# GpSimd's products of the causal convolution: tensor times one scalar per partition in place of tensor times a stretched weight

## The chip, the cores and the metric

The kernel runs on one core of a Trainium2 chip. A core has several engines with queues of their own: TensorE (PE in the profile; its weight loads are listed apart as PEld), VectorE (DVE), ScalarE (ACT), GpSimd (POOL) and SyncE (SP), which here issues most DMAs. Each engine works through its own list of instructions in order; semaphores hold an instruction until what it reads is there. The metric is device time in microseconds (us) of one execution. The numbers for the kernel before are from three timed runs and one profiled execution.

## The reference, cut to what matters

An attention with a causal mask and a decay bias (batch 8, heads 8, 576 tokens, 64 per head) gives `x` of 576 tokens by 512 channels per batch. It goes through a gated linear unit whose gate is a causal depthwise convolution of five taps:

```python
xp = np.concatenate([np.zeros((B, K - 1, D)), x], axis=1)
gate_pre = np.zeros((B, S, D))
for k in range(K):                                   # K = 5
    gate_pre += conv_w[k][None, None, :] * xp[:, k:k + S, :]
gate = 1.0 / (1.0 + np.exp(-gate_pre))
val = x @ w_val
return gate * val @ w_out
```

For one channel a tap is one number for all tokens. In the kernel channels lie on partitions and tokens along them, so a tap is one scalar per partition.

## The kernel before, in words

The work is cut into 32 units `n` (8 batches of 4 pairs of heads; a pair of heads is 128 channels, one full set of partitions). For each unit the kernel loads Q, K and V, casts Q and K to bf16 (`c_q`, `c_k`), transposes them on TensorE (`qt`, `qq`) and copies them out of PSUM (`qe`); TensorE makes scores (`s0` to `s2`, `s4`), ScalarE their exponentials (`e0` to `e2`, `e4`), GpSimd masks the diagonal blocks of some units (`mk`, `ml`, L580) and multiplies V by the exponential of the decay (`vp`, L475); TensorE multiplies by V (`av0`, `av`, L595), VectorE normalises (`rec`, `nm`), and TensorE turns the result so that channels lie on partitions (`xt`, L627). That result stands in PSUM as bf16 and is copied to SBUF as `xT` (`xe`).

The convolution of unit `n` then runs over up to 576 tokens. `t1` (L666, VectorE) adds tap 1 to the unshifted value; the weights are divided by the last tap beforehand (`cwr`), so that the last tap costs nothing here. Taps 2, 3 and 4 come either from VectorE in one instruction, product and sum (L671), or from GpSimd in two: a product `p2`, `p3` or `p4` written to one of two buffers `pr` in f32, and the sum `t2`, `t3` or `t4` of `gp` and `pr` (L674). Some products are made by ScalarE (L653). The function of the products is `tap_product`. ScalarE then takes the tanh (`th`), TensorE the value product (`val`, L704), VectorE the gate times the value (`glu`), and TensorE the output product (`out`, L724). The last batch (units 28 to 31) is done in two halves of 384 and 192 tokens, with shorter products.

What runs where and in which order is written out by hand in one long string, `ORDER`: a list of steps `name.index:engine:buffer`, where G is GpSimd, V VectorE, A ScalarE, T TensorE and S SyncE. Each engine's instructions are issued in the order of that list. GpSimd's list has 29 products, 37 sums, 32 products of V, 19 masks and 16 casts, one after the other; a piece of it around units 5 and 6 reads (other engines' steps left out):

```
t2.5:G  cast_wo:G  t3.5:G  p3.6:G:0  mk.9:G  p4.5:G:1  t3.6:G  t4.5:G  vp.2.0:G
```

Of the kernel before, what the change touches and what calls it, by code (L numbers as in the profile page):

```python
# [12 lines left out]
ALU = mybir.AluOpType  # L13
# [284 lines left out]
def main_path(ctx, tc, q, k, v, s, moe_w_val, moe_conv_w, moe_w_out, out, okcnt):  # L298
# [6 lines left out]
    vec, act, pool, sync, pe = nc.vector, nc.scalar, nc.gpsimd, nc.sync, nc.tensor  # L305
# [35 lines left out]
    xTs = many("xT", [128, 4, 4 + S], BF16)  # L341
# [304 lines left out]
    def tap_product(m):  # L646
        def f(e, n, *h):
            b, c = divmod(n, 4)
            lo, hi = span(*h)
            lo = max(lo, m)  # L650
            pr, r = prs[at[f"p{m}", n, *h][0]][:, lo:hi], cwr[:, c, 4 - m:5 - m]
            if e is act:
                act.activation(out=pr, in_=xps(n, *h)[:, lo - m:hi - m], func=AF.Copy, scale=r)  # L653
            else:
                pool.tensor_tensor(pr, xTs[b % 2][:, c, 4 + lo - m:4 + hi - m], r.to_broadcast([128, hi - lo]),  # L655
                                   ALU.mult)
        return f

    def tap(m):
# [181 lines left out]
```

## Time and profile before

| what | value |
| --- | --- |
| median of three runs | 189.03 us (188.85 to 191.28) |
| time of the profiled execution | 188.3 us |
| span of the profiled execution, first to last instruction | 186.5 us |
| busy: PE, ACT, DVE, POOL | 173.7, 171.3, 165.3, 162.1 us |
| GpSimd's products (L655) | 29, 29.7 us busy |
| GpSimd's sums (L674) | 37, 46.1 us busy |
| ScalarE's products of the same kind (L653) | 8 |

The span lies 1.8 us under the time of its execution, and that execution 0.7 us under the median of the runs. Busy times are sums over the span; an engine's list is in order, so an engine that is busy nearly throughout can make others late even where the chain that ended last doesn't name it.

### The profile page before, as it was taken

The numbers are of one execution on the slowest core, as the hardware profiler recorded it, in microseconds if no ns is written. First come the engines' busy times: TensorE is split into PE (matmuls) and PEld (weight loads), VectorE is DVE, ScalarE is ACT, GpSimd is POOL, SyncE is SP. The second block draws the span as 40 slices with busy tenths as digits, with TensorE's granted clock in tenths as the row PEclk, the third lists the DMA queues.
The fourth block names the chain that finished last, engine by engine and source line by source line (L and its number), as shares of the span: only waits on it lengthen the run. The fifth ranks groups of instructions, "written<-read, shape, count | busy, mean of one in ns | idle before, by whom it ended". The sixth has DMA issues, their size and how long they took to land.

```text
span 186.5 us, 6691 instructions
## 1 busy us (share of the span) xinstructions
PE 173.7 (93%) x2735; PEld 114.3 (61%) x2735; DVE 165.3 (89%) x320; ACT 171.3 (92%) x233; POOL 162.1 (87%) x145
## 2 busy tenths in 40 slices
PE   6999797889999999999979999999999999999991
PEld 2547574377757665576845676486666865667560
DVE  4876989879998899998999999989999899999980
ACT  3399979999999989999999989999999999999871
POOL 5049999998999999999999999799999988799530
PEclk9999999999999999999999999999999999999998
DMA  5999999899899999997999992899970003403064
GB/s 181 238 292 317 241 270 195 235 361 302 173 303 350 396 250 251 257 339 193 301 201 241 330 295 75 251 292 283 201 248 3 4 5 112 169 5 116 2 225 176
DMA packets 62283, 40.46 MB, mean 217 GB/s; under 512 B 47333, under 2 KB 49381, under 8 KB 62250
## 3 DMA queue, kind: packets, MB, share of 16 engines
q1 hardware_dynamic: 61706, 39.49, 76.8%
q8 instruction: 22, 0.36, 0.8%
q10 hardware_dynamic: 544, 0.52, 0.8%
q14 instruction: 11, 0.09, 0.2%
HBM read 30.57 MB, written 9.44 MB: 214 GB/s over the span
## 4 chain that ended last, share of the span: by engine, by line
PE 72%; ACT 18%; DVE 4%; issue 3%; POOL 0%; ACTq 0%; POOLq 0%; DVEq 0%
PE bank L704 15%; PE bank L724 15%; PE bank L595 13%; ACT P L557 13%; PE bank L506 11%; PE bank L621 6%; PE bank L627 4%; PE bank L630 3%; PE bank L490 2%; PE bank L519 1%; PE bank L481 1%; ACT ot L374 1%; DVE gp L666 1%; DVE gp L671 1%; ACT th L691 1%
## 5 line engine op out<-in xcount | busy, mean ns | idle before, releaser
L557 ACT ACTIVATE P<-bank 128x1024 bf16<-128x1024 f32 x84 | 83.2, 1044 | 3.3 <-PE bank L506 1.9
L671 DVE SCALAR_TENSOR_TENSOR gp<-bank,cwr,gp 128x574 f32<-128x574 bf16 (+6 forms) x71 | 51.2, 743 | 0.3
L674 POOL TENSOR_TENSOR gp<-gp,pr 128x572 f32<-128x572 f32 (+6 forms) x37 | 46.1, 1249 | 4.8 <-DVE gp L671 2.9
L506 PE MATMUL bank<-QKT 64*128 64x128 bf16 (+4 forms) x592 | 38.1, 237 | 4.5 <-ACT P L557 2.5
L475 POOL TENSOR_TENSOR Vp<-vst,w 128x650 bf16<-128x650 f32 x32 | 40.6, 1288 | 0.2 <-ACT w L395 0.2
L704 PE MATMUL bank<-xT,wv 128*128 128x288 bf16 (+2 forms) x256 | 38.2, 286 | 0.9 <-DVE gp L671 0.5
L595 PEld LDWEIGHTS <-P 128*128 128x128 bf16 x960 | 33.2, 97 | 6.0 <-issue 1.6
L595 PE MATMUL bank<-Vp,P 128*128 128x65 bf16 x960 | 36.2, 194 | 0.8 <-ACT P L557 0.6
L724 PE MATMUL bank<-wo,glu 128*128 128x512 bf16 x144 | 36.0, 380 | 0.0
L506 PEld LDWEIGHTS <-QKT 64*128 64x128 bf16 x592 | 19.3, 94 | 22.1 <-issue 16.4
L655 POOL TENSOR_TENSOR pr<-xT,cwr 128x572 f32<-128x572 bf16 (+6 forms) x29 | 29.7, 1031 | 2.0 <-DVE xT L374 0.9
L704 PEld LDWEIGHTS <-wv 128*128 128x128 bf16 x256 | 22.5, 97 | 9.9 <-issue 3.8
L713 DVE SCALAR_TENSOR_TENSOR glu<-th,bank 128x288 bf16<-128x288 f32 (+2 forms) x64 | 26.9, 446 | 1.7 <-ACT th L691 0.5
L666 DVE SCALAR_TENSOR_TENSOR gp<-xT,cwr,bank 128x576 f32<-128x576 bf16 (+2 forms) x36 | 26.6, 743 | 1.2 <-ACT xT L374 0.2
L614 DVE TENSOR_TENSOR xn<-bank,recs 128x640 bf16<-128x640 f32 (+2 forms) x36 | 26.9, 747 | 0.7
L580 POOL TENSOR_SCALAR_AFFINE_SELECT P<-P 128x1024 bf16<-128x1024 bf16 (+2 forms) x19 | 19.2, 1011 | 9.2 <-ACT P L557 9.1
L374 ACT COPY QKT<-bank 128x1024 bf16<-128x1024 bf16 (+1 forms) x21 | 20.9, 1027 | 2.2 <-PE bank L490 2.1
L691 ACT ACTIVATE th<-gp,cwr 128x576 f32<-128x576 f32 x28 | 21.8, 799 | 0.0
L724 PEld LDWEIGHTS <-glu 128*128 128x128 bf16 x144 | 12.1, 98 | 12.6 <-issue 1.9
L374 ACT COPY ot<-bank 128x512 f32<-128x512 f32 x29 | 17.2, 610 | 1.8 <-PE bank L724 1.7
L374 DVE COPY QKT<-bank 128x1024 bf16<-128x1024 bf16 (+1 forms) x15 | 14.5, 972 | 3.7 <-PE bank L490 2.4
L627 PE MATMUL bank<-ident,xn 128*128 128x128 bf16 x164 | 15.0, 220 | 0.9 <-ACT P L557 0.6
(66 smaller groups left out, 184.2 us busy)
## 6 DMA issues: line engine op xcount, KB each, us to landing
out_dram<-ot SPq DMA_DIRECT2D x36, 256.0 KB, 3.1
vst<-in_v_dram SPq DMA_DIRECT2D x28, 256.0 KB, 6.4
first<-in_q_dram SPq DMA_DIRECT2D x6, 512.0 KB, 6.8
first<-in_k_dram SPq DMA_DIRECT2D x6, 512.0 KB, 7.4
qkf<-in_q_dram SPq DMA_DIRECT2D x6, 512.0 KB, 7.1
qkf<-in_k_dram SPq DMA_DIRECT2D x6, 512.0 KB, 6.7
vst<-in_v_dram SPq DMA_DIRECT2D x15, 128.0 KB, 4.8
first<-in_q_dram SPq DMA_DIRECT2D x4, 256.0 KB, 4.0
```

Source lines behind the costliest of these rows:

```text
L374: (act.copy if e is act else e.tensor_copy)(dst, src)
L475: e.tensor_tensor(Vps[b % 2][:, :, HP[p]], vslot(b)[:, :, HP[p]], w[:, :, b * 8 + 2 * p:b * 8 + 2 * p + 2].unsqueeze(3).to_broadcast([128, ...
L506: pe.matmul(ps[:, hh, c0:c0 + nq], QKTs[b % 2][r, 1, p, k0:k0 + 128], QKTs[b % 2][r, 0, p, q0:q0 + nq], **kw)
L557: act.activation(out=Pt(n)[:, :, step * 512:(step + 1) * 512], in_=pair((f"s{step}", n)), func=AF.Exp, scale=0.125)
L595: pe.matmul(ps[:, o:o + 65], lhsT, Vps[b % 2][:, kb, 2 * p + w, :], start=(kb == 0), stop=(kb == qb))
L614: vec.tensor_tensor(xns[b % 2][:, g, p * 128:(p + 1) * 128].rearrange("t g (w d) -> t w g d", w=2), ps[:, :, :, 0:64], recs[:, n, :, g].un ...
L655: pool.tensor_tensor(pr, xTs[b % 2][:, c, 4 + lo - m:4 + hi - m], r.to_broadcast([128, hi - lo]), ALU.mult)
L666: vec.scalar_tensor_tensor(gp[:, lo:hi], xT[:, 3 + lo:3 + hi], r, xps(n, *h)[:, lo:hi], ALU.mult, ALU.add)
L671: vec.scalar_tensor_tensor(gp[:, lo:hi], xps(n, *h)[:, lo - m:hi - m], r, gp[:, lo:hi], ALU.mult, ALU.add)
L674: pool.tensor_tensor(gp[:, lo:hi], gp[:, lo:hi], prs[at[f"p{m}", n, *h][0]][:, lo:hi], ALU.add)
L704: pe.matmul(ps, wv[:, dc, c * 128:(c + 1) * 128], xTs[b % 2][:, dc, 4 + lo:4 + hi], start=(dc == 0), stop=(dc == 3))
L724: pe.matmul(bank_of(u, i), glu2[:, c, i * 128:i * 128 + 128], wo[:, c, :], start=(c == 0), stop=(c == 3))
```

## The change

In `tap_product`, the branch for GpSimd changes. Before, it is `tensor_tensor`: two tensor operands, the second being the weight `r` (one f32 number per partition) stretched over the 192 to 574 tokens by a step of zero. After, it is `tensor_scalar`: one tensor operand, and `r` given as the scalar operand, one f32 per partition; its second operation is left empty. Input (bf16 `xT`), output (f32 `pr`), the numbers of elements, the buffers and `ORDER` stay as they are. ScalarE's branch and the sums stay too.

```diff
             if e is act:
                 act.activation(out=pr, in_=xps(n, *h)[:, lo - m:hi - m], func=AF.Copy, scale=r)
             else:
-                pool.tensor_tensor(pr, xTs[b % 2][:, c, 4 + lo - m:4 + hi - m], r.to_broadcast([128, hi - lo]),
-                                   ALU.mult)
+                pool.tensor_scalar(pr, xTs[b % 2][:, c, 4 + lo - m:4 + hi - m], r, None, ALU.mult)
         return f
```

## The prediction

> **What bounds the kernel now.** I read the busy shares first, then the chain that ended last, and then asked what GpSimd's list, which the change touches, does to that chain.
>
> ```profile
> PE 173.7 (93%) x2735; PEld 114.3 (61%) x2735; DVE 165.3 (89%) x320; ACT 171.3 (92%) x233; POOL 162.1 (87%) x145
> PE 72%; ACT 18%; DVE 4%; issue 3%; POOL 0%; ACTq 0%; POOLq 0%; DVEq 0%
> ```
>
> The first line is busy time and its share of the span by engine, the second the shares of the chain. TensorE carries the chain and ScalarE most of the rest; GpSimd has nothing in it. So a faster GpSimd has nothing of its own to take off the end. That doesn't make a slower GpSimd free: the table of two stretches (from:to, length, then each engine's busy us) shows how full it is.
>
> ```profile
> 20.00:140.00 120.00, 113.34 (x1971) 76.16 (x1970) 111.18 (x194) 116.60 (x148) 117.30 (x91) 1.00 0.97 263
> 140.00:180.00 40.00, 39.83 (x556) 26.94 (x551) 38.79 (x90) 38.28 (x64) 34.07 (x36) 1.00 0.19 68
> ```
>
> The columns of busy time are PE, PEld, DVE, ACT, POOL. From 20 to 140 us GpSimd is busy for 117.30 of 120 us, more than any other engine there, and idles for 2.7; from 140 to 180 it idles for 5.9. The view of waits says who is kept waiting by it, and whom it waits for (total us, times, longest).
>
> ```profile
> PEld L595 <- POOL Vp L475: 0.7, 1, 0.7
> ACT P L557 <- POOL pr L655: 0.3, 1, 0.3
> PE bank L595 <- POOL Vp L475: 0.2, 1, 0.2
> ...
> POOL P L580 <- ACT P L557: 9.1, 3, 5.7
> POOL gp L674 <- DVE gp L671: 2.9, 4, 1.7
> POOL gp L674 <- DVE gp L666: 1.2, 2, 0.8
> POOL pr L655 <- DVE xT L374: 0.9, 2, 0.6
> POOL pr L655 <- ACT xT L374: 0.7, 1, 0.7
> ```
>
> Others wait for GpSimd for 1.2 us in all. The timeline (start, length, engine, line) shows what these waits are worth, and how near the others come:
>
> ```profile
> 22.96 1.28 POOL L475 TENSOR_TENSOR Vp<-vst,w 128x650 bf16<-128x650 f32 x1
> 23.30 1.05 ACT L557 ACTIVATE P<-bank 128x1024 bf16<-128x1024 f32 x1
> 24.49 0.70 PE L595 MATMUL bank<-Vp,P 128*128 128x65 bf16 x18 [0.41 <-ACT P L557]
> ...
> 26.41 0.40 PE L506 MATMUL bank<-QKT 64*128 64x128 bf16 x8
> 26.91 2.13 ACT L557 ACTIVATE P<-bank 128x1024 bf16<-128x1024 f32 x2 [0.30 <-POOL pr L655]
> ...
> 35.60 3.76 POOL L475 TENSOR_TENSOR Vp<-vst,w 128x650 bf16<-128x650 f32 x3
> 36.94 1.08 PE L595 MATMUL bank<-Vp,P 128*128 128x65 bf16 x30
> 38.17 0.49 PE L595 MATMUL bank<-Vp,P 128*128 128x65 bf16 x11 [0.16 <-POOL Vp L475]
> 48.33 1.89 POOL L374 CAST wo<-qkf 128x2048 bf16<-128x2048 f32 x1
> 50.27 1.02 PE L724 MATMUL bank<-wo,glu 128*128 128x512 bf16 x4
> 178.95 0.59 POOL L674 TENSOR_TENSOR gp<-gp,pr 128x192 f32<-128x192 f32 x1 [0.46 <-DVE gp L671]
> 179.72 0.41 DVE L671 SCALAR_TENSOR_TENSOR gp<-bank,cwr,gp 128x192 f32<-128x192 bf16 x1
> ```
>
> The wait of 0.7 us, of a weight load, ends with the product of V at 22.96 + 1.28 = 24.24, but the matmul behind it also needs exponentials that end at 24.35. The one of 0.3 us is followed by an exponential at 26.91 whose scores are only done at 26.81. That leaves the 0.2 us, at 38.17.
>
> The output weights are cast by 48.33 + 1.89 = 50.22, and TensorE's first output product starts at 50.27: 0.05 us later. The last sum on GpSimd ends at 179.54, 0.18 us before VectorE goes on with that `gp`. A delay of GpSimd reaches TensorE almost at once, and TensorE, busy for 113 of 120 us, hardly catches up.
>
> **The change, part by part.** It swaps 29 instructions; none is added, moved or dropped, no DMA and no wait. Those removed, by shape (count | busy us, mean ns | idle before):
>
> ```profile
> L655 POOL TENSOR_TENSOR pr<-xT,cwr 128x572 f32<-128x572 bf16 x10 | 11.4, 1140 | 0.2
> L655 POOL TENSOR_TENSOR pr<-xT,cwr 128x574 f32<-128x574 bf16 x7 | 8.0, 1142 | 1.0 <-DVE xT L374 0.9
> L655 POOL TENSOR_TENSOR pr<-xT,cwr 128x573 f32<-128x573 bf16 x5 | 5.7, 1139 | 0.0
> L655 POOL TENSOR_TENSOR pr<-xT,cwr 128x380 f32<-128x380 bf16 x2 | 1.6, 818 | 0.0
> L655 POOL TENSOR_TENSOR pr<-xT,cwr 128x192 f32<-128x192 bf16 x3 | 1.5, 505 | 0.8 <-ACT xT L374 0.7
> ```
>
> 22 are full-length at 1.14 us, 4 have 380 to 382 elements (818 to 824 ns, one row shown) and 3 have 192. By elements that is 22 + 4 x 381/573 + 3 x 192/573 = 25.7 full-length products. From 192 to 572 elements 635 ns pass: 1.67 ns an element over a fixed 184 ns.
>
> The new form, one tensor and one scalar per partition, isn't in GpSimd's list before. The nearest rows are its instructions with one tensor input, and as the other end those with two:
>
> ```profile
> L374 POOL CAST qkb<-qkf 128x2048 bf16<-128x2048 f32 x6 | 11.3, 1891 | 0.2 <-DMA qkf<-in_k_dram 0.2
> L374 POOL CAST qkb<-qkf 128x1024 bf16<-128x1024 f32 x2 | 2.1, 1036 | 0.1
> L580 POOL TENSOR_SCALAR_AFFINE_SELECT P<-P 128x1024 bf16<-128x1024 bf16 x16 | 17.5, 1094 | 9.2 <-ACT P L557 9.1
> L580 POOL TENSOR_SCALAR_AFFINE_SELECT P<-P 128x256 bf16<-128x256 bf16 x2 | 0.8, 420 | 0.0
> L674 POOL TENSOR_TENSOR gp<-gp,pr 128x572 f32<-128x572 f32 x14 | 19.6, 1402 | 0.7 <-DVE gp L671 0.5
> ```
>
> Cast: (1891 - 1036)/1024 = 0.835 ns an element over 181 ns. Mask: (1094 - 420)/768 = 0.88 over 195. Both have one tensor input and cost half of the stretched product's slope; the sum, with two f32 inputs, is dearer than the product. Low end, by the cast: 181 + 573 x 0.835 = 660 ns. High end: if the instruction's two operations, of which one is left empty, were two passes, a product and one at the sum's price, 1140 + 1402 = 2542 ns. I take 0.66 to 0.70, by the rows nearest in kind (one tensor input, the mask even working out a value per element), and keep 2.54 for the range.
>
> At 0.66 a full-length product saves 0.48 us, all of them 25.7 x 0.48 = 12.3 us of GpSimd. What is that worth? Of the waits for GpSimd, the rows above leave 0.2 us that end with it alone: I take **0.2 us off**. The other 12 us become idle time: GpSimd reaches the masks and sums sooner and waits there for ScalarE's exponentials and VectorE's taps (the rows above with POOL as the waiting engine grow). What is late next is TensorE itself. Earlier casts free the buffers of Q and K sooner; no row above has an engine other than GpSimd waiting on that.
>
> Sum: 188.3 - 0.2 = 188.1 us against the profiled execution's own time; the median of the runs shown lies 0.7 us above that execution, so **188.8 us** as a median.
>
> There is a price at which the sign turns; it hangs on how much of GpSimd's idle time lies ahead of the first product.
>
> ```profile
> 9.23 1.09 POOL L580 TENSOR_SCALAR_AFFINE_SELECT P<-P 128x1024 bf16<-128x1024 bf16 x1 [5.70 <-ACT P L557]
> 13.50 1.09 POOL L580 TENSOR_SCALAR_AFFINE_SELECT P<-P 128x1024 bf16<-128x1024 bf16 x1 [2.39 <-ACT P L557]
> ```
>
> GpSimd can swallow added work only in its idle time after the first product: from the rows, 2.9 + 1.2 + 0.9 + 0.7 and, of the 9.1 for masks, the 1.0 that is neither of these two: 6.7 us. The rest reaches TensorE, by the 0.05 us distances above. So x us more per full-length product cost between 25.7x - 6.7 and 25.7x. Up to 1.14 us nothing is lost; 2% of 188.3 is 3.8 us, reached at x between 0.15 and 0.41, a price of 1.29 to 1.55 us.
>
> **The rivals.** The first needs one more row, the sum at 192 elements:
>
> ```profile
> L674 POOL TENSOR_TENSOR gp<-gp,pr 128x192 f32<-128x192 f32 x5 | 3.0, 592 | 1.9 <-DVE gp L666 1.2 <-DVE gp L671 0.5
> ```
>
> *The scalar form is dear on GpSimd* (slower). One mechanism: the instruction's own loop, not its inputs, sets the pace. For it: the trace has not one such instruction on this engine, and the two-input forms already differ (product 1.67, sum (1402 - 592)/380 = 2.13 ns an element), so a form's price can't be read from its number of inputs alone. Against it: both one-input forms run below 0.9. At the sum's price, 1.40 us: 25.7 x 0.26 = 6.7 us more work, 0 to 6.7 at the end, about 191.7. Halfway, 1.97 us: 21.3 more, 14.6 to 21.3, about 206. At 2.54: 36.0 more, 29.3 to 36.0, about 221. It decides from about 1.4 us a product on.
>
> [...]
>
> [...]
>
> *GpSimd is the hidden pace* (faster). If short distances like the one at 50.27 are waits in truth that the view doesn't list, TensorE could use part of its idle 120 - 113.3 = 6.7 us: at best 188.3 - 6.7 = 181.6, half of it 185. Against it: POOL's share of the chain is 0%.
>
> *Nothing changes*, since the engine runs both forms alike: 1.14 us, 188.3 profiled, 189.0 as a median.
>
> **How the numbers follow.** Forecast, with prices from the low end up to 1.1 us: 0.48, around 188.8. Nothing changes: 0.05. The dear form: 0.41, of which a tenth stays within 2%. First call: 0.02. Hidden pace: 0.04. So 2% faster, about the least that a measurement of this kernel tells from no change: 0.04; within 2%: 0.48 + 0.05 + 0.04 = 0.57; slower by more: 0.37 + 0.02 = 0.39. The dear form gets so much because its price is a guess from other instructions and because GpSimd has no room. The range runs from 187.3 (all 1.2 us of waits gone, and the runs' spread) to 210, which holds the dear form up to about 2.1 us a product; about 0.17 is left out above and 0.03 below. The likeliest case's own range is 187.3 to 190.5, since the runs before reach from 188.85 to 191.28.
>
> **What would show it.** In the groups after: L655 as a one-input instruction at 650 to 700 ns full-length, 17.4 us in all against 29.7; GpSimd's busy time near 150; its waits for P and gp larger by about 12 us; TensorE's busy time and chain as before. If the price is over 1.4 us, GpSimd would be near 95% busy, PE would wait for Vp and wo, and "POOL" would enter the chain. What would make the forecast wrong is that one price above all.

## The result: 5% slower

The changed kernel takes 198.86 us in the median of four runs (198.79 to 199.87), the kernel before 189.18 (188.85 to 191.28): 1.050 times as long, with a 95% interval of 1.042 to 1.058. The forecast was 188.8 us and no change that can be told. The profiled execution took 198.79 us, span 197.1; 10.5 us more than that of before.

The rows that answer to those shown of before: the changed kernel's products by shape (count | busy us, mean ns | idle before).

```profile
L655 POOL TENSOR_SCALAR pr<-xT,cwr 128x572 f32<-128x572 bf16 x10 | 17.2, 1718 | 0.2
L655 POOL TENSOR_SCALAR pr<-xT,cwr 128x574 f32<-128x574 bf16 x7 | 12.2, 1737 | 0.6 <-DVE xT L374 0.6
L655 POOL TENSOR_SCALAR pr<-xT,cwr 128x573 f32<-128x573 bf16 x5 | 8.6, 1728 | 0.0
L655 POOL TENSOR_SCALAR pr<-xT,cwr 128x380 f32<-128x380 bf16 x2 | 2.5, 1244 | 0.0
L655 POOL TENSOR_SCALAR pr<-xT,cwr 128x192 f32<-128x192 bf16 x3 | 2.3, 765 | 0.2
```

A full-length product takes 1.72 us where the stretched one took 1.14 and 0.66 was forecast. From 192 to 572 elements it is (1718 - 765)/380 = 2.51 ns an element over 283 ns. The busy shares, the shares of the chain that ended last and the two stretches show what that does (columns of busy time: PE, PEld, DVE, ACT, POOL):

```profile
PE 174.9 (89%) x2735; PEld 114.9 (58%) x2735; DVE 165.9 (84%) x320; ACT 173.0 (88%) x233; POOL 177.6 (90%) x145
...
PE 8%; POOL 3%; DVE 2%; ACT 0%; issue 0%; ACTq 0%
```

```profile
20.00:140.00 120.00, 107.33 (x1863) 72.10 (x1861) 104.71 (x181) 110.31 (x139) 119.07 (x85) 1.00 0.94 252
140.00:180.00 40.00, 36.50 (x544) 24.36 (x540) 35.66 (x74) 36.83 (x53) 39.20 (x31) 1.00 0.22 72
```

GpSimd has 177.6 - 162.1 = 15.5 us more to do and its idle time from 20 to 180 us falls from 8.6 to 1.7 us. TensorE's total hardly changes (173.7 before, 174.9 now), but in the first stretch it is busy for 107.3 us where it was 113.3: it waits. The chain could be followed back over only 13% of the span here; GpSimd, absent before, has 3 of these 13. The view of waits names who is kept waiting by GpSimd, ScalarE's tanh and then TensorE (total us, times, longest; a matmul, PE, and its weight load, PEld, are listed apart, so one wait can stand in both; lines behind L655 have moved up by one, the sums from L674 to L673):

```profile
ACT th L690 <- POOL gp L673: 4.5, 6, 1.3
...
PEld L595 <- POOL P L580: 2.9, 4, 0.9
...
PE bank L595 <- POOL Vp L475: 2.4, 4, 1.0
...
PE bank L595 <- POOL P L580: 1.8, 3, 0.8
...
PEld L630 <- POOL qkb L374: 1.6, 2, 1.0
...
PE bank L630 <- POOL qkb L374: 1.3, 2, 0.8
...
PE bank L723 <- POOL wo L374: 0.6, 1, 0.6
```

None of these waits for a product itself. Behind a dearer product everything else on GpSimd's list comes later: masks, products of V, casts, sums. The two places of before with the short distances, in the timeline of the changed kernel:

```profile
37.30 3.77 POOL L475 TENSOR_TENSOR Vp<-vst,w 128x650 bf16<-128x650 f32 x3
38.64 1.08 PE L595 MATMUL bank<-Vp,P 128*128 128x65 bf16 x30 [1.01 <-POOL Vp L475]
...
50.67 1.89 POOL L374 CAST wo<-qkf 128x2048 bf16<-128x2048 f32 x1
52.61 1.67 PE L723 MATMUL bank<-wo,glu 128*128 128x512 bf16 x7 [0.58 <-POOL wo L374]
```

The products of V start at 37.30 (before 35.60), the cast of the output weights ends at 52.56 (before 50.22), and now TensorE waits at both.

### The profile page after: what moved, and what is told of

It is laid out like the page before. It is cut to its first block, busy times and chain, and to the rows that moved or that the text cites. A ratio compares the mean times of both kernels' runs of the same rounds, so it can differ in the third digit from the quotient of the medians.

```text
span 197.1 us, 6691 instructions
## 1 busy us (share of the span) xinstructions
PE 174.9 (89%) x2735; PEld 114.9 (58%) x2735; DVE 165.9 (84%) x320; ACT 173.0 (88%) x233; POOL 177.6 (90%) x145
## 5 line engine op out<-in xcount | busy, mean ns | idle before, releaser
L673 POOL TENSOR_TENSOR gp<-gp,pr 128x572 f32<-128x572 f32 (+6 forms) x37 | 46.0, 1248 | 2.0 <-DVE gp L665 0.8
L655 POOL TENSOR_SCALAR pr<-xT,cwr 128x572 f32<-128x572 bf16 (+6 forms) x29 | 45.2, 1561 | 1.1 <-DVE xT L374 0.6
L506 PE MATMUL bank<-QKT 64*128 64x128 bf16 (+4 forms) x592 | 37.6, 237 | 7.9 <-ACT P L557 5.5
L723 PEld LDWEIGHTS <-glu 128*128 128x128 bf16 x144 | 12.3, 98 | 13.3 <-issue 2.5
L608 DVE RECIPROCAL recs<-bank 128x10 f32<-128x10 f32 (+2 forms) x36 | 7.6, 211 | 10.5 <-PE bank L595 8.2
```

Source lines behind the costliest of these rows:

```text
L506: pe.matmul(ps[:, hh, c0:c0 + nq], QKTs[b % 2][r, 1, p, k0:k0 + 128], QKTs[b % 2][r, 0, p, q0:q0 + nq], **kw)
L655: pool.tensor_scalar(pr, xTs[b % 2][:, c, 4 + lo - m:4 + hi - m], r, None, ALU.mult)
L673: pool.tensor_tensor(gp[:, lo:hi], gp[:, lo:hi], prs[at[f"p{m}", n, *h][0]][:, lo:hi], ALU.add)
L723: pe.matmul(bank_of(u, i), glu2[:, c, i * 128:i * 128 + 128], wo[:, c, :], start=(c == 0), stop=(c == 3))
```

## The experiments

The theory was: the loss is the scalar form's own time on an engine with almost no idle time, and of the prediction only the price was wrong. The rivals: something beside GpSimd's time (what the form holds or disturbs), neighbours that stretch it, the scalar's coming from memory, the empty second operation.

**Plain copies in place of the products.**

```diff
-                pool.tensor_scalar(pr, xTs[b % 2][:, c, 4 + lo - m:4 + hi - m], r, None, ALU.mult)
+                pool.tensor_copy(pr, xTs[b % 2][:, c, 4 + lo - m:4 + hi - m])
```

> GpSimd's products become plain copies of xT to f32 (the multiplication by the weight is left out, all else is as before). This is the price that the prediction assumed for the scalar form. Theory 'price' (the loss is the scalar form's own 1.72 us against 1.14, on an engine with hardly any idle time; only that step of the prediction was wrong): a copy of 572 elements takes 0.65 to 0.70 us, GpSimd's busy time falls to about 150 us, and the time is that of before within 0.5 us. Rival 'neighbours' (whatever one-input form stands here is stretched by what the other engines do beside it): the copy takes over 1 us too. Rival 'hidden pace': the copy is short and the time falls by 2 us or more.

188.73 us, 0.9988 times before (0.9963 to 1.0014). Of this run, a row of the groups by shape, the busy shares and the rows of GpSimd's waits for masks, sums and products:

```profile
L655 POOL CAST pr<-xT 128x572 f32<-128x572 bf16 x10 | 6.6, 661 | 0.5 <-ACT xT L374 0.3
```

```profile
PE 173.3 (92%) x2719; PEld 114.4 (61%) x2735; DVE 164.6 (87%) x320; ACT 171.4 (91%) x233; POOL 150.0 (80%) x145
```

```profile
POOL P L580 <- ACT P L557: 10.9, 6, 5.1
POOL gp L673 <- DVE gp L670: 6.6, 6, 2.2
...
POOL pr L655 <- DVE xT L374: 2.7, 3, 1.8
...
POOL pr L655 <- ACT xT L374: 2.4, 3, 1.5
...
POOL gp L673 <- DVE gp L665: 1.8, 3, 1.0
...
POOL P L580 <- ACT P L571: 1.2, 1, 1.2
```

A one-input copy does cost 0.66 us here beside all the other work, GpSimd's busy time falls to 150.0 us, and the time doesn't move. So the step from price to time held at the price that the forecast took: the freed 12 us become GpSimd's own waits. Those ahead of masks grow from 9.1 to 12.1 us and those ahead of sums from 4.1 to 8.4, 7.3 together, where the prediction had all 12; those ahead of the products grow too, from 1.6 to 5.1, which it did not name. The rivals 'neighbours' and 'hidden pace' are out.

**Only the delay.** The kernel before, with the stretched products, and a sum of two scratch tiles behind each.

```diff
                 pool.tensor_tensor(pr, xTs[b % 2][:, c, 4 + lo - m:4 + hi - m], r.to_broadcast([128, hi - lo]),
                                    ALU.mult)
+                k = {192: 57, 380: 137, 381: 137, 382: 137}.get(hi - lo, 207)
+                pool.tensor_tensor(scr[:, 0:k], scr[:, 0:k], scr2[:, 0:k], ALU.add)
```

> The kernel before, with its stretched products, and behind each of the 29 a sum on GpSimd of two scratch tiles that nobody reads, sized so that product and scratch sum together take as long as the scalar form does (207 elements behind a full-length product, 137 and 57 behind the shorter ones). Theory 'price': GpSimd's time is all that counts, so this is as slow as the changed kernel: 198 to 200 us, GpSimd busy for about 178 us. Rival 'form' (the scalar form costs the others something beside GpSimd's time, say by what it holds while it runs): clearly under 198, towards 189.

199.17 us, 1.053 times before (1.051 to 1.055), against 198.86 for the changed kernel. Its busy shares and the shares of its chain that ended last:

```profile
PE 174.2 (88%) x2719; PEld 115.2 (58%) x2735; DVE 166.7 (84%) x322; ACT 173.0 (88%) x233; POOL 177.0 (90%) x174
...
PE 34%; POOL 33%; DVE 11%; ACT 7%; DMA 6%; issue 6%; SPq 1%; POOLq 0%; ACTq 0%; DVEq 0%
```

With no scalar form in it at all, the same time on GpSimd (177.0 us) gives the same loss, and GpSimd stands in the chain that ended last with 33%, where before it had 0. So GpSimd's time alone is enough to explain the loss.

**One half at a time.**

```diff
+                x = xTs[b % 2][:, c, 4 + lo - m:4 + hi - m]
+                if n < 16:                                  # in the other run: n >= 16
+                    pool.tensor_scalar(pr, x, r, None, ALU.mult)
+                else:
+                    pool.tensor_tensor(pr, x, r.to_broadcast([128, hi - lo]), ALU.mult)
```

> The scalar form in units 0 to 15 alone (12 full-length products), the stretched one from unit 16 on. It adds 12 x 0.58 = 7.0 us to GpSimd, where its idle time between 20 and 100 us is about 1 us. Theory 'price': 5 to 7 us over before, 194 to 196 us; nothing given back later. If the lateness were made up in the second half: under 192.

> The scalar form from unit 16 on alone (10 full-length and 7 shorter products), the stretched one before. It adds about 10 x 0.58 + 4 x 0.43 + 3 x 0.26 = 8.3 us to GpSimd, which in the kernel before idles for some 6 us in that stretch. Theory 'price': 2.5 to 5 us over before, 191.5 to 194 us, less than the first half's although more is added; the two halves together about the whole, 10 us. If idle time didn't matter: 8 us over before.

194.82 us for the first half (1.031 times before, 1.029 to 1.033) and 193.10 for the second (1.020, 1.017 to 1.023), with 189.08 for before beside them: 5.7 and 4.0 us, together 9.8, the whole. GpSimd's busy times are 169.4 and 170.5 us, so the smaller addition cost more, 5.7 of 7.3 us against 4.0 of 8.4. That fits the idle time that the prediction read from the kernel before: 2.7 us from 20 to 140 us, 5.9 from 140 to 180. Nothing of the first half's lateness was made up later: in the profiles, ScalarE's exponential that starts at 100.59 us before starts at 107.03 with the first half changed, 6.4 us later, and its last copy is 6.4 us late too (182.42 and 188.87). (The profiled execution of before was 0.8 us under the median of its runs, so 6.4 us here answers to 5.7 there.)

**The prices by themselves.** GpSimd alone, with nothing of the attention or the convolution computed; three of each at 572 and at 192 elements (eleven forms ran, one fewer than the expectation says).

```python
pool.tensor_tensor(p, x, r.to_broadcast([128, n]), ALU.mult)   # L49
pool.tensor_scalar(p, x, r, None, ALU.mult)                    # L51, the change's form
pool.tensor_scalar(p, x, 0.75, None, ALU.mult)                 # L53, an immediate number
pool.tensor_scalar(p, x, r, 0.5, ALU.mult, ALU.add)            # L55, second operation filled
pool.tensor_copy(p, x)                                         # L57
pool.tensor_scalar(p, f, r, None, ALU.mult)                    # L59, f32 input
...
pool.tensor_scalar(p, x, r, None, ALU.add)                     # L63
pool.tensor_tensor(g, g, p, ALU.add)                           # L65
```

> None of the attention or the convolution is computed: GpSimd alone runs twelve forms three times each at 572 and at 192 elements on constant tiles, the other engines idle (zeros are written out). Theory 'loop' (the instruction's own code on GpSimd costs 2.5 ns an element over 0.28 us, whatever stands beside it and wherever the scalar comes from): the scalar form with the weight from memory takes 1.72 us here too, with an immediate number the same within 5%, with a second operation (add 0.5) filled in the same within 5%, with add in place of mult the same. Rival 'pointer': with an immediate number it falls to the copy's 0.66 us. Rival 'second operation': it is dearer by another 0.5 us or more when the second operation is filled. Rival 'neighbours': the scalar form takes 0.66 to 1.1 us when the other engines idle. Both: stretched product 1.14, copy 0.66, sum of two f32 1.40. Open, to see if a cheaper pair of product and sum exists: f32 in place of bf16 input, bf16 in place of f32 output, and a sum whose second input is bf16.

The groups by shape of this run; the line number tells the form:

```profile
L63 POOL TENSOR_SCALAR pr<-xT,cwr 128x572 f32<-128x572 bf16 x3 | 5.2, 1719 | 0.3
...
L59 POOL TENSOR_SCALAR pr<-xf,cwr 128x572 f32<-128x572 f32 x3 | 5.1, 1715 | 0.3
L51 POOL TENSOR_SCALAR pr<-xT,cwr 128x572 f32<-128x572 bf16 x3 | 5.1, 1714 | 0.2
L53 POOL TENSOR_SCALAR pr<-xT 128x572 f32<-128x572 bf16 x3 | 4.9, 1639 | 0.3
L65 POOL TENSOR_TENSOR gp<-gp,pr 128x572 f32<-128x572 f32 x3 | 4.2, 1388 | 0.2
...
L49 POOL TENSOR_TENSOR pr<-xT,cwr 128x572 f32<-128x572 bf16 x3 | 3.4, 1141 | 3.5 <-DVE cwr L43 3.5
...
L55 POOL TENSOR_SCALAR pr<-xT,cwr 128x572 f32<-128x572 bf16 x3 | 2.2, 746 | 0.3
...
L57 POOL CAST pr<-xT 128x572 f32<-128x572 bf16 x3 | 2.0, 663 | 0.2
...
L55 POOL TENSOR_SCALAR pr<-xT,cwr 128x192 f32<-128x192 bf16 x3 | 1.3, 429 | 0.3
```

Alone, the change's form (L51) takes 1.714 us, as in the kernel; an immediate number saves 0.08 us, f32 input and add in place of mult change nothing (1.715 and 1.719). So neither the scalar's place nor the input sets the pace. But the expectation for the filled second operation was wrong: with "add 0.5" the instruction takes 0.746 us, less than half. Its slope is (746 - 429)/380 = 0.83 ns an element, the copy's, which takes 346 ns at 192 elements: (663 - 346)/380 = 0.83.

**Which pairs are cheap.** Again GpSimd alone.

```python
pool.tensor_scalar(p, x, r, 0.0, ALU.mult, ALU.add)       # L50
pool.tensor_scalar(p, x, r, 1.0, ALU.mult, ALU.mult)      # L52
pool.tensor_scalar(p, x, r, z, ALU.mult, ALU.add)         # L54, z from memory
pool.tensor_scalar(p, x, 0.75, 0.5, ALU.mult, ALU.add)    # L56
pool.tensor_scalar(p, x, r, 9.0, ALU.mult, ALU.min)       # L58
pool.tensor_scalar(p, x, r, 0.5, ALU.add, ALU.mult)       # L60
pool.tensor_scalar(p, x, r, 0.0, ALU.mult, ALU.subtract)  # L62
pool.tensor_scalar(p, x, r, None, ALU.max)                # L64
...
```

> Again GpSimd alone, nothing of the attention computed; nine scalar forms three times each at 572 and 192 elements. In the run before, a scalar form took 1.72 us with its second operation empty and 0.75 us with the second operation 'add 0.5' filled in: filling it made it cheaper, which no theory had. Theory 'one pair' (the code knows multiply-then-add, and takes a slow way for the rest): mult then add takes 0.75 us with 0.0, with the addend from memory, with both numbers immediate and with bf16 output, and all other pairs (mult mult, mult min, add mult, mult subtract, max alone) take 1.6 us or more. Theory 'empty second operation' (only the missing second operation is slow): every filled pair takes about 0.75 us, max alone 1.7.

The groups by shape, at 572 elements:

```profile
L62 POOL TENSOR_SCALAR pr<-xT,cwr 128x572 f32<-128x572 bf16 x3 | 6.6, 2198 | 0.3
L58 POOL TENSOR_SCALAR pr<-xT,cwr 128x572 f32<-128x572 bf16 x3 | 6.6, 2192 | 0.3
L64 POOL TENSOR_SCALAR pr<-xT,cwr 128x572 f32<-128x572 bf16 x3 | 5.1, 1712 | 0.3
...
L54 POOL TENSOR_SCALAR pr<-xT,cwr,zz 128x572 f32<-128x572 bf16 x3 | 2.4, 814 | 0.2
...
L52 POOL TENSOR_SCALAR pr<-xT,cwr 128x572 f32<-128x572 bf16 x3 | 2.2, 742 | 0.0
L50 POOL TENSOR_SCALAR pr<-xT,cwr 128x572 f32<-128x572 bf16 x3 | 2.2, 742 | 3.6 <-DVE zz L44 3.6
...
L60 POOL TENSOR_SCALAR pr<-xT,cwr 128x572 f32<-128x572 bf16 x3 | 2.2, 742 | 0.3
L56 POOL TENSOR_SCALAR pr<-xT 128x572 f32<-128x572 bf16 x3 | 2.0, 668 | 0.3
```

Both theories miss. Three prices appear: the pairs mult-add, mult-mult and add-mult take 0.74 us (0.67 with immediates, 0.81 with both scalars from memory, and mult-add with bf16 output 0.74 as well), one operation alone 1.71, and mult followed by min or by subtract 2.19. Neither "one pair" nor "any filled pair" is right; of the pairs tried, those of mult and add alone are cheap. Why one operation is dearer than two wasn't tried further; no run shows what makes it so.

**The second operation filled in the kernel.**

```diff
-                pool.tensor_scalar(pr, xTs[b % 2][:, c, 4 + lo - m:4 + hi - m], r, None, ALU.mult)
+                pool.tensor_scalar(pr, xTs[b % 2][:, c, 4 + lo - m:4 + hi - m], r, 0.0, ALU.mult, ALU.add)
```

> The changed kernel with the second operation filled: times r, plus 0.0, the same result as the changed kernel's. Theory 'price': a product takes 0.75 us in the kernel too, GpSimd's busy time falls to about 152 us, and as in the run with plain copies the time is that of before within 0.5 us: 188.5 to 189.3 us, all of the changed kernel's 10 us gone. If anything about a scalar operand other than its time mattered, it would stay above 190.

188.90 us, 0.9992 times before (0.9969 to 1.0016). The 10 us are gone. A row of its groups, its busy shares and the shares of its chain:

```profile
L655 POOL TENSOR_SCALAR pr<-xT,cwr 128x572 f32<-128x572 bf16 x10 | 7.5, 748 | 0.6 <-ACT xT L374 0.4
```

```profile
PE 173.1 (92%) x2719; PEld 114.9 (61%) x2735; DVE 164.6 (88%) x320; ACT 171.5 (92%) x233; POOL 153.0 (82%) x145
...
PE 70%; ACT 19%; DVE 4%; issue 4%; POOL 0%; ACTq 0%; POOLq 0%; DVEq 0%
```

GpSimd is 9 us less busy than before and 0.39 us faster per product, and the chain is as before: TensorE 70%, ScalarE 19%, GpSimd 0. A cheaper GpSimd by itself is worth nothing that these runs can tell.

**Spending the freed time.** As the last one, and ScalarE's 8 products handed to GpSimd, by their letters in `ORDER` (`p4.1:A:1` becomes `p4.1:G:1`, and so on).

> As scalar_mult_add, and the 8 products that ScalarE makes (0.77 us each, 6 us in all) are made by GpSimd at the same places in the list. It spends what the cheaper form frees on GpSimd (10 us) to take 6 us off ScalarE, which carries 18% of the chain of before. If ScalarE's time is worth its share, 0.5 to 1.5 us under before: 187.5 to 188.5 us. If TensorE sets the end alone, no difference: 188.7 to 189.3. If the moved products come too late for the sums that wait for them, slower than 189.5.

190.19 us, 1.0064 times before (1.0038 to 1.0089): a little slower, and over the 189.5 of the expectation's third case. Its busy shares and two rows of its waits:

```profile
PE 172.1 (91%) x2719; PEld 114.3 (61%) x2735; DVE 165.8 (88%) x320; ACT 167.7 (89%) x225; POOL 157.9 (84%) x153
```

```profile
PE bank L595 <- POOL Vp L475: 1.4, 3, 0.9
...
PEld L595 <- POOL Vp L475: 0.7, 1, 0.7
```

ScalarE is 171.3 - 167.7 = 3.6 us less busy than before, not 6, and TensorE's matmuls wait 1.4 us for products of V, which now stand behind the moved products in GpSimd's list. In the kernel before it was 0.2 us (the 0.7 of the weight loads stood there too), and in the run without the moves no wait for them is listed. The third case had the sums come late; the rows show mostly the products of V. That the places in the list are the cause is argued from these waits; another placing wasn't tried. No version tried beats the kernel before by more than its measurement is uncertain.

## Why the prediction was wrong, by its own steps

- **The price of the form: the step that failed.** The prediction took 0.66 to 0.70 us "by the rows nearest in kind". Measured: 1.72 us in the kernel, 1.71 alone. A saving of 25.7 x 0.48 = 12.3 us became an addition of 25.7 x 0.58 = 14.9 us (15.5 in GpSimd's busy time). The rows of copy and mask say what those instructions cost, not what an instruction with the same inputs and another operation costs. The trace itself held the warning, which the rival named: the two two-input forms differ by a quarter in slope (1.67 and 2.13 ns an element).
- **Its high end had a wrong reason.** It thought of the empty second operation as a second pass, 2.54 us. With the second operation empty the instruction took 1.71 us; filled with add or mult it was cheaper (0.74), with min or subtract dearer (2.19).
- **What a price is worth in time: held, but as a wide range.** The prediction's rule gives, for 0.58 us more, between 25.7 x 0.58 - 6.7 = 8.2 and 14.9 us; measured 10.5 in the profiled executions, 9.7 in the medians. Of the 6.7 us of idle time that it took as the most that could swallow added work, 15.5 - 10.5 = 5.0 did. For 0.66 and 0.75 us it gives almost nothing; measured ratios 0.9988 and 0.9992, both with 1 inside their intervals. For 1.14 plus a delay of 0.58, the same as for 1.72: 199.17.
- **Where it would show: held in the main.** The prediction said that a price over 1.4 us would put GpSimd near 95% busy, with TensorE waiting for Vp and wo and POOL in the chain. GpSimd is at 90% of the longer span, 99% between 20 and 140 us. Both waits are there, with those for the masks and for the casts of Q and K, which it hadn't named; so are ScalarE's 4.5 us for sums. POOL is in the chain, of which the changed kernel's profile shows only the end; over the whole span the run with only the delay shows it, at 33%.
- **One reading was short.** "Others wait for GpSimd for 1.2 us in all" leaves out the 1.4 us that TensorE waits at the start for the identity matrix that GpSimd makes. That wait lies ahead of the first product and is 1.4 us after the change as well, so no number of the forecast hangs on it.
- **The rivals.** *The dear form* came true, and half of its mechanism fits: the price hangs on the operations that the instruction is given (0.74, 1.71 or 2.19 us), while input type (1.714 us with bf16, 1.715 with f32) and the scalar's place (1.639 as an immediate number) hardly matter. That a loop of the instruction sets the pace was the author's guess; what in the engine makes it so, no run shows. The turning price of about 1.4 us wasn't measured; 1.72 lies beyond it. *First call*, to which the prediction gave 0.02 (the first of the new instructions costs more than those behind it): no run shows such a surcharge. The first scalar product, in the changed kernel's timeline, takes 1.74 us, as all seven of its shape do in the mean (1.737). The first stretched product of before took its shape's mean too (1.14), and the first three products of V there took 3.94 us, 1.31 each against a mean of 1.29 over all 32. The first row is of the changed kernel, the others of before:

```profile
20.78 1.74 POOL L655 TENSOR_SCALAR pr<-xT,cwr 128x574 f32<-128x574 bf16 x1
...
20.80 1.14 POOL L655 TENSOR_TENSOR pr<-xT,cwr 128x574 f32<-128x574 bf16 x1
...
14.76 3.94 POOL L475 TENSOR_TENSOR Vp<-vst,w 128x650 bf16<-128x650 f32 x3 [0.17 <-ACT w L395]
...
L475 POOL TENSOR_TENSOR Vp<-vst,w 128x650 bf16<-128x650 f32 x32 | 40.6, 1288 | 0.2 <-ACT w L395 0.2
```

- *Hidden pace*: no, GpSimd with 12 us less leaves the time where it was. *Nothing changes*: no, the two forms differ by 0.58 us a product.
- **The chances.** 0.39 for slower was too little for a term whose two ends lay a factor of four apart on an engine that the prediction had itself found full. The likeliest value of an unknown price was taken where the loss on the dear side was large and the gain on the cheap side 0.2 us.

## What to carry to other kernels

Read what an engine off the critical path could still take before anything is put on it: here it idled for 8.6 us of 160, and of 15.5 us added only 5.0 were swallowed; 10.5 reached the end. A form that isn't in the trace has no price there, even if its inputs look like those of one that is; measure it alone, in one run, before the list is planned around it. Of the three ways tried in this kernel, a product with one scalar per partition on GpSimd is cheapest as times r, plus 0 (0.75 us), then as a stretched tensor (1.14), and dearest as times r alone (1.72).

## What the runs showed of the hardware that was not expected

On GpSimd, at 572 elements, one operation with a scalar took 1.71 us, multiply-then-add 0.74 and multiply-then-min 2.19: the number of operations doesn't order the prices. Nor do the slopes follow it: from 192 to 572 elements the copy rose by 0.83 ns an element, multiply-then-add (0.5) by 0.83 as well, and one operation alone by (1714 - 766)/380 = 2.49. In the kernel before, a weight stretched by a zero step was cheaper as a second input (1.67 ns an element) than a second f32 tensor, added (2.13); whether the step, the type or the operation makes that difference wasn't separated, beyond a sum with a bf16 second input that took 1.27 us where the one with f32 took 1.39.

```profile
L51 POOL TENSOR_SCALAR pr<-xT,cwr 128x192 f32<-128x192 bf16 x3 | 2.3, 766 | 0.0
...
L57 POOL CAST pr<-xT 128x192 f32<-128x192 bf16 x3 | 1.0, 346 | 0.2
...
L67 POOL TENSOR_TENSOR gp<-gp,prb 128x572 f32<-128x572 f32 x3 | 3.8, 1266 | 0.1
```

The lines are from the run of prices by themselves: the change's form and the copy at 192 elements, and its line 67, `pool.tensor_tensor(g, g, pb, ALU.add)` with `pb` in bf16.
